# First chunk's softmax of taps issued ahead of the weights' loads, last four tokens in twos, and a new order of steps

## The chip, the cores and the metric

The kernel runs on one core of one Trainium2 chip. The metric is the device time in microseconds (us); the kernel before takes 1347.68 us (median of 3 runs, 1347.58 to 1349.73). Five engines work from queues of their own: PE (matrix products; PEld is its loading of weights), DVE (vector), ACT (scalar functions), POOL (GpSimd) and SP, which here only issues transfers. Each engine takes its instructions in the order in which they were written into its queue.

## The reference, cut to what matters

```
w   = softmax(weight_gen, axis=-1)            # 8 x 4160 x 8 heads x 7 taps
x   = einsum(w, last 7 rows of x_in)          # causal, 24 columns per head, 192 in all
h   = x @ w_in                                # 33280 x 192 by 192 x 1024
s   = h * softmax(h, axis=-1)
ln  = (s - mean(s)) / sqrt(var(s) + 1e-6) * g_ln
out = ln @ w_out                              # 33280 x 1024 by 1024 x 192
```

## The kernel before, in words

The 33280 rows are cut into 128 runs of 260, one run on each partition. A *token* t (0 to 259) is one row of every run, so one token is one 128-row tile of the products. Tokens are loaded in *chunks* that start at 0, 4, 12, 20, 36 and then every 16 up to 244.

For each chunk there is a softmax of the taps in seven steps (`softmax_taps`, t0 to t6): DVE takes the maximum (L112), POOL subtracts it (L114), ACT takes the exponential (L118), DVE sums (L120), ACT copies (L122), DVE takes the reciprocal (L124) and POOL multiplies (L126). For each *group* of tokens POOL then forms the seven products and adds them in part (attA and attB: L174, L180, L182 into `half`), DVE makes the last sum (fin, L433, into `a`) and ACT copies some columns (dup, L439). A group is 4 tokens; only the first four tokens go in two groups of 2 (`group`).

For each pair of tokens PE transposes `a` (xT, L450), ACT rounds it (xhi, L458) and DVE makes the rest (xld, L479, into `x_lo`). For each token follow, in this order: mm1 on PE (L491, L494 into a slot `h` of three in PSUM), max on DVE (L505), exp on ACT (L509), solu on DVE (L515), hi on ACT (L528), sq on ACT (L521), lo on DVE (L532), tr (a transposing transfer issued by SP, L540, `hlT`), mm2 on PE (L580) and out on ACT (L591). Steps sq and lo of one token never run at once. mm1 of token t needs sq and lo of token t-3. The scales of the output (f0 to f5, three small steps on ACT and three on DVE, L552 to L567) are made for 4 tokens at a time, for 2 among the first eight (`stat_group`); a store (L594) follows each fourth token.

At the start the weights come in as 64-bit numbers in `raw_a`, `raw_b` and `raw_2` and are converted in seven parts (a0, b, a1, c0 to c3) on DVE and ACT, L241 to L260, 512 or 384 columns each. Loads are issued on the queues of SP and of ACT (L76 to L90, L96, L195, L196, L202, L206). The steps of chunk 0's softmax of taps are written at L227, behind all of these loads.

From L640 on the steps are issued in the order that `issue_order` returns. It is a planner: each step has an engine, a cost in ns, and the steps it needs; some have a time before which they are not taken up (`ready`), each engine has a time at which it is free first (`free`), and among the steps that an engine could take the one with the smallest t + `URGENCY` goes first. The planner's order becomes the order of each engine's queue.

Of the kernel before, what the change touches and what calls it, by code (L numbers as in the profile page):

```python
# [26 lines left out]
def tile_kernel(ctx: ExitStack, tc: tile.TileContext, x, weight_gen, w_in, w_out, g_ln, out):  # L27
# [9 lines left out]
    RUN = B * S // P  # L37
    PB = P // B
    TG = 4
# [27 lines left out]
    def load_x(c, part=0):  # L67
        t0, n = starts[c], starts[c + 1] - starts[c]
        if part == 0:
            xs[c] = io.tile([P, (TC + HALO) * D], F32, name="xt")  # L70
        xt = xs[c]
        xv = xt.rearrange("p (t d) -> p t d", d=D)
        if c == 0:

            nc.gpsimd.memset(xt[:, : HALO * D], 0.0)
            nc.sync.dma_start(xv[:, HALO : HALO + n, :], x_run[:, :n, :])  # L76
            for b in range(B):
                queue = nc.sync if b % 2 else nc.scalar
                queue.dma_start(
                    xv[b * PB + 1 : (b + 1) * PB, :HALO, :],  # L80
                    x_run[b * PB : (b + 1) * PB - 1, RUN - HALO :, :],
                )
        elif t0 < HALO:
            first = xs[0].rearrange("p (t d) -> p t d", d=D)
            nc.sync.dma_start(xv[:, HALO : HALO + n, :], x_run[:, t0 : t0 + n, :])
            nc.sync.dma_start(xv[:, :HALO, :], first[:, t0 : t0 + HALO, :])
        else:
            cuts = [(HALO + n) * k // LOADS for k in range(LOADS + 1)]
            r0, r1 = cuts[part], cuts[part + 1]
            nc.sync.dma_start(xv[:, r0:r1, :], x_run[:, t0 - HALO + r0 : t0 - HALO + r1, :])  # L90
# [9 lines left out]
    TAP_STEPS = 7  # L100

    def softmax_taps(c, step):
        n = (starts[c + 1] - starts[c]) * H
        w3 = ws[c][:, : n * K].rearrange("p (n k) -> p n k", k=K)
        if step == 0:
            m = small.tile([P, TC * H], F32, name="wm", bufs=2)[:, :n]
            y = small.tile([P, TC * H], F32, name="wy", bufs=2)[:, :n]
            taps[c] = m, y
        m, y = taps[c]
        wide = [P, n, K]  # L110
        if step == 0:
            nc.vector.tensor_reduce(m, w3, axis=AX.X, op=ALU.max)  # L112
        elif step == 1:
            nc.gpsimd.tensor_tensor(  # L114
                out=w3, in0=w3, in1=m.unsqueeze(2).broadcast_to(wide), op=ALU.subtract
            )
        elif step == 2:
            nc.scalar.activation(w3, w3, AF.Exp)  # L118
        elif step == 3:
            nc.vector.tensor_reduce(m, w3, axis=AX.X, op=ALU.add)  # L120
        elif step == 4:
            nc.scalar.activation(y, m, AF.Copy, bias=1e-9)  # L122
        elif step == 5:
            nc.vector.reciprocal(y, y)  # L124
        elif step == 6:
            nc.gpsimd.tensor_tensor(  # L126
                out=w3, in0=w3, in1=y.unsqueeze(2).broadcast_to(wide), op=ALU.mult
            )
# [59 lines left out]
    w_in = w_in.bitcast(I32)  # L188
    w_out = w_out.bitcast(I32)
    load_x(0)  # L190
    raw_a = att.tile([P, 2 * FF], I32, name="raw_a", bufs=1)

    raw_b = big.tile([P, FF], I32, name="hl", bufs=3)
# [29 lines left out]
    column = const.tile([P, 1], F32, name="column")  # L223
    minus = const.tile([P, P], F32R, name="minus")
    nc.vector.tensor_scalar_mul(minus, ident, -1.0)

    for step in range(TAP_STEPS):  # L227
        softmax_taps(0, step)

    scratch = {}  # L230

# [173 lines left out]

    def stat_group(t):

        n = 2 if t < 2 * TG else TG
        return n if t % n == n - 1 else 0


    def group(t):

        if t < TG:
            return 2 if t % 2 == 0 else 0
        return TG if t % TG == 0 else 0

# [225 lines left out]


URGENCY = dict(
    a00=3.1, a01=2.3, a02=-28.9, a03=-6.5, a04=-3.6, a10=80, a11=-25.4, a12=-13, a13=-10, a14=10.4,
    attA=85.1, attB=2.4, b0=120.9, b1=-144.6, b2=138.3, b3=-1.5, b4=54.3, c00=-28.1, c01=85.1,
    c02=6.8, c10=-25.3, c11=31.3, c12=-72.7, c20=99.4, c21=-5.6, c22=10.2, c30=-149.7, c31=-14.5,
    c32=-100.3, dup=52.6, exp=-129.5, f0=8.2, f1=-120.4, f2=-71.5, f3=-118.4, f4=-66.1, f5=-45.6,
    fin=18.4, hi=-11, lo=33, lw=18.7, lx0=10.2, lx1=-115.4, lx2=-109.1, lx3=-20.7, max=-30,  # L650
    mm1=25.5, mm2=0.4, n0=-7.5, n1=11.8, n2=-1.8, n3=-113.6, n4=-8.6, n5=-69, n6=-123.6, od=-6.9,
    out=-81.2, p30=22.9, p31=0.5, p4=9.7, p5=12.6, p6=11.6, p70=-10.2, p71=-8.7, p80=20.3, p81=5.9,
    q00=7.1, q01=-5.1, q02=118.9, q10=-15.7, q11=20.7, q12=16.8, q20=100.6, q21=-95.2, q22=20.4,
    q30=143.8, q31=81.5, q32=98.3, solu=-7.6, sq=5, t0=5.1, t1=-3.7, t2=77.9, t3=44.1, t4=-26.5,
    t5=110.1, t6=267.2, tr=-13, v00=170.9, v01=5.1, v02=44, v03=0.2, v1=54.2, v2=58.8, v3=-12.2,
    v4=1, v5=21.2, xT=-66.9, xhi=-46.7, xld=30,
)


def issue_order(run, starts, group, stat_group, loads):  # L660
# [5 lines left out]

    PE, DVE, ACT, SP, POOL = range(5)
    SAME, CROSS = (25, 127, 143, 0, 102), 130
    free = [3000, 5900, 5000, 12000, 9050]
    steps, number = [], {}  # L670

    def add(name, t, engine, cost, *after, ready=0):
# [3 lines left out]
    def once(name, engine, cost, *after, ready=0):  # L676
        add(name, 0, engine, cost, *((x, 0) for x in after), ready=ready)
# [2 lines left out]
    parts = ["a0", "b", "a1", *(f"c{f}" for f in range(4))]  # L680
    for n, part in enumerate(parts):
        w_in, size = n < 3, 512 if n < 3 else 384
        at = (9000, 10500, 12000)[n] if w_in else 15000
        before = () if w_in else (f"{parts[n - 3]}4", "n" + {"a0": "0", "a1": "1", "b": "2"}[parts[n - 3]]) if n < 6 else ("q00",)
        if n:
            before += (parts[n - 1] + "0",)
        once(part + "0", DVE, 3 * (60 + size), *before, ready=at)
        once(part + "1", ACT, 2 * (190 + 0.85 * size), part + "0")
        once(part + "2", DVE, 3 * (60 + 1.04 * size), part + "1")
        if w_in:  # L690
            once(part + "3", ACT, 190 + 0.75 * size, part + "2")
            once(part + "4", DVE, 60 + 1.04 * size, part + "3")
            once("n" + {"a0": "0", "a1": "1", "b": "2"}[part], DVE, 60 + 1.04 * size, part + "2")
        else:
            f = n - 3
            once(f"q{f}0", ACT, 700, part + "2")
            once(f"q{f}1", PE, 660, f"q{f}0", *([f"q{f - 1}1"] if f else ["n6"]))
            once(f"q{f}2", ACT, 520, f"q{f}0")
    add("p30", 0, DVE, 868, ("q31", 0), ("mm1", 1))
# [31 lines left out]
        add("v4", t, DVE, 80, ("v3", t))  # L731
        add("v5", t, ACT, 240, ("v4", t))

    add("v00", 0, ACT, 1800, ready=9000)
    add_norms(0, 0)
    for c in range(1, len(starts) - 1):
        t, before = starts[c], starts[c - 1] if c > 1 else -1
        short = starts[c + 1] - t < 16
        if c > 1:
            add("lw", t, SP, 1270, last_group(c - 3))  # L740
            add("lx0", t, SP, 1540, last_group(c - 2), *parts_of(c - 2))
            for n in range(1, loads):
                add(f"lx{n}", t, SP, 1540, (f"lx{n - 1}", t))
        whole = starts[c + 1] - t == 16
        for part in range(4 if whole else 1):
            size = 830 if whole else 1800
            if c > 1:

                load = min(part + 1, loads - 1) if whole else loads - 1
                add(f"v0{part}", t, ACT, size, (f"lx{load}", t))  # L750
            else:
                add(f"v0{part}", t, ACT, size, ready=15000)
        add_norms(c, t)
        n = (starts[c + 1] - t) * 8
        on = (DVE, POOL, ACT, DVE, ACT, DVE, POOL)
        wide = 60 + 7.3 * n
        costs = (wide, 13.5 * n, 100 + 6 * n, wide, 100 + n, 60 + 6.3 * n, 13.5 * n)
        for k in range(7):
            if k:
                add(f"t{k}", t, on[k], costs[k], (f"t{k - 1}", t))  # L760
            elif c > 1:
                add("t0", t, on[k], costs[k], ("lw", t), ("t6", before))
            else:
                add("t0", t, on[k], costs[k], ready=12000)


    groups = [t for t in range(run) if group(t)]
# [1 line left out]
    for i, t in enumerate(groups):  # L769
        c, full = chunk_of(t), group(t) == 4  # L770
        after = [("attB", groups[i - 1])] if i else []
        if c:
            after.append(("t6", starts[c]))
        if c > 1:
            after.append((f"lx{loads - 1}", starts[c]))
        add("attA", t, POOL, 14990 if full else 7500, *after, ready=15000 if c == 1 else 9000)
        add("attB", t, POOL, 3510 if full else 1800, ("attA", t), ("fin", groups[i - 2] if i > 1 else -1))
        old = t // 4 * 4 - 12
        add("dup", t, ACT, 307 if full else 200, ("fin", t))
        add("fin", t, DVE, 1710 if full else 880, ("attB", t), ("xT", old + 2 if old >= 0 else -1))  # L780
# [144 lines left out]
```

## Time and profile before

| | |
|---|---|
| median of 3 runs | 1347.68 us |
| the profiled execution | 1347.67 us, of which the span from first to last instruction is 1345.8 us |
| granted PE clock, mean | 0.994 |
| max of token 0 starts at | 50.59 us |
| POOL's last sum (L182) starts at | 1286.95 us, 3.48 us long |
| last store issued at | 1342.58 us |

A row of the waits view reads "engine line waited for: total us, times, longest us". A row of a timeline reads "start, duration, engine, line, operation, out<-in, shapes, count, and in brackets the idle time ahead of it with what ended it"; ACTq and SPq rows are issues of transfers. A row of the windows view gives a stretch in us, its length, the busy time of PE, PEld, DVE, ACT and POOL (with counts), the granted PE clock, the busy share of the transfer engines and GB/s.

### The profile page before, as it was taken

What the parts mean: (1) busy time and instruction counts of PE and PEld (TensorE: products, weight loads), DVE (VectorE), ACT (ScalarE), POOL (GpSimd) and SP (SyncE); (2) the same over time, 40 slices, a digit from 0 to 9 for tenths busy, and PEclk for the clock granted to TensorE, in tenths of its full rate; (3) what the DMA queues carried; (4) which work ended last, traced back from release to release, by engine and by line L of the source; (5) the groups of instructions that cost most, each with busy time, mean ns of one, the idle gap of its engine ahead of it and who ended that gap; (6) DMA issues with size and microseconds to landing.
All of it is one profiled execution on the core that took longest, in us unless ns stands there. A gap on an engine that the chain in (4) does not pass through costs nothing.

```text
span 1345.8 us, 25810 instructions
## 1 busy us (share of the span) xinstructions
PE 1246.8 (93%) x9900; PEld 970.8 (72%) x9900; DVE 1210.2 (90%) x1588; ACT 1162.8 (86%) x2318; POOL 1247.7 (93%) x241
## 2 busy tenths in 40 slices
PE   0588899999999999999999999999999999999997
PEld 0365677777777777777777777777777777777776
DVE  5988899999999999999999999999999999889994
ACT  3778889889898988989898998989898898988886
POOL 5989899999999999999999999999999999999930
PEclk9899999999999999999999999999999999999999
DMA  5277668797886889688797968878787877976776
GB/s 180 74 159 169 139 134 201 123 207 137 155 179 134 196 137 208 125 179 163 129 202 140 191 140 180 162 128 203 140 193 137 183 150 138 183 134 123 133 134 130
DMA packets 565307, 210.31 MB, mean 156 GB/s; under 512 B 544456, under 2 KB 545864, under 8 KB 565184
## 3 DMA queue, kind: packets, MB, share of 16 engines
q1 hardware_dynamic: 563208, 206.55, 75.7%
q10 hardware_dynamic: 1976, 2.12, 0.6%
q8 instruction: 78, 1.28, 0.4%
q14 instruction: 45, 0.37, 0.1%
HBM read 46.15 MB, written 25.56 MB: 53 GB/s over the span
## 4 chain that ended last, share of the span: by engine, by line
ACT 43%; DVE 35%; issue 11%; PE 7%; DMA 2%; POOL 1%; SPq 0%; ACTq 0%; POOLq 0%
ACT hl L528 12%; ACT e L521 12%; DVE h L515 11%; DVE hl L532 11%; ACT e L509 9%; DVE stats L505 5%; DVE a L433 4%; ACT junk L145 3%; PE po L580 3%; PE h L494 2%; ACT x_hi L458 2%; ACT ot L591 2%; DMA hlT<-hl 2%; PE h L491 1%; DVE x_lo L479 1%
## 5 line engine op out<-in xcount | busy, mean ns | idle before, releaser
L174 POOL TENSOR_TENSOR pr<-xt,wt 128x5376 f32<-128x5376 f32 (+1 forms) x66 | 631.6, 9569 | 2.7
L580 PE MATMUL po<-w_hl,hlT 128*128 128x192 f16 x6192 | 555.1, 246 | 17.3 <-ACT ot L591 12.6
L580 PEld LDWEIGHTS <-hlT 128*128 128x128 f16 x6240 | 505.9, 98 | 83.2 <-issue 75.5
L515 DVE SCALAR_TENSOR_TENSOR h<-h,row,e 128x1024 f32<-128x1024 f32 x260 | 333.8, 1285 | 19.1 <-ACT e L509 16.9
L528 ACT ACTIVATE hl<-h 128x1024 f16<-128x1024 f32 x260 | 266.0, 1029 | 98.4 <-DVE h L515 55.4
L532 DVE SCALAR_TENSOR_TENSOR hl<-h,hl 128x1024 f16<-128x1024 f32 x260 | 316.5, 1218 | 36.8 <-ACT e L521 34.4
L180 POOL TENSOR_TENSOR pr<-pr 128x2304 f32<-128x2304 f32 (+1 forms) x66 | 333.0, 5045 | 5.2
L505 DVE TENSOR_REDUCE stats<-h 128x1 f32<-128x1024 f32 x260 | 316.3, 1217 | 3.9 <-PE h L494 3.3
L509 ACT ACTIVATE e<-h,stats 128x1024 f32<-128x1024 f32 x260 | 293.3, 1128 | 16.1 <-DVE stats L505 15.5
L521 ACT ACTIVATE e<-h,stats 128x1024 f32<-128x1024 f32 x260 | 293.0, 1127 | 1.1 <-DVE hl L532 1.0
L494 PE MATMUL h<-wa_hi,x_hi 128*128 128x512 f32 x520 | 234.0, 450 | 0.0
L182 POOL TENSOR_TENSOR half<-pr 128x1536 f32<-128x1536 f32 (+1 forms) x66 | 225.8, 3421 | 5.2
L494 PE MATMUL h<-wa_lo,x_hi 128*128 128x512 f32 x520 | 206.4, 397 | 0.0
L494 PE MATMUL h<-wa_hi,x_lo 128*128 128x512 f32 x520 | 205.9, 396 | 0.0
L494 PEld LDWEIGHTS h<-wa_hi,x_hi 128*128 128x128 f32 x520 | 98.1, 189 | 107.1 <-issue 95.5
L491 PE MATMUL h<-wb_hi,x_hi 64*128 64x512 f32 x520 | 131.0, 499 | 17.1 <-DVE hl L532 11.2
L433 DVE TENSOR_REDUCE a<-half 128x768 f32<-128x1536 f32 (+1 forms) x66 | 117.2, 1776 | 0.0
L591 ACT ACTIVATE ot<-po,stats 128x192 f32<-128x192 f32 x258 | 112.4, 436 | 3.6 <-PE po L580 3.6
L494 PEld LDWEIGHTS h<-wa_hi,x_lo 128*128 128x128 f32 x520 | 98.4, 189 | 23.2
L494 PEld LDWEIGHTS h<-wa_lo,x_hi 128*128 128x128 f32 x520 | 99.0, 190 | 12.0
L491 PE MATMUL h<-wb_hi,x_lo 64*128 64x512 f32 x520 | 104.2, 395 | 0.0
L450 PE MATMUL pa<-ident,a 128*128 128x128 f32 x520 | 81.2, 278 | 23.9 <-DVE x_lo L479 13.2
(89 smaller groups left out, 1072.0 us busy)
## 6 DMA issues: line engine op xcount, KB each, us to landing
out_dram<-ot SPq DMA_DIRECT2D x65, 384.0 KB, 3.3
xt<-in_x_dram SPq DMA_DIRECT2D x30, 576.0 KB, 4.8
xt<-in_x_dram SPq DMA_DIRECT2D x30, 480.0 KB, 4.4
wt<-in_weight_gen_dram SPq DMA_DIRECT2D x15, 448.0 KB, 4.8
hlT<-hl SPq DMA_TRANSPOSE x260, 4.7
xt<-in_x_dram SPq DMA_DIRECT2D x3, 384.0 KB, 4.6
raw_a<-in_moe_w_in_dram ACTq DMA_DIRECT2D x2, 512.0 KB, 7.4
raw<-in_moe_w_out_dram ACTq DMA_DIRECT2D x1, 768.0 KB, 12.2
```

Of the source, the lines that this page charges most:

```text
L174: nc.gpsimd.tensor_tensor(out=window(pr, 0, [(TG * D, K), (HG, n * H), (1, HG)]), in0=window(xt, t * D, [(D, K), (HG, n * H), (1, HG)]), i ...
L180: nc.gpsimd.tensor_tensor(out=pr[:, :3], in0=pr[:, :3], in1=pr[:, 3:6], op=ALU.add)
L182: nc.gpsimd.tensor_tensor(out=half, in0=window(pr, 0, [(2 * TG * D, 2), (D, n), (1, D)]), in1=window(pr, TG * D, [(5 * TG * D, 2), (D, n), ...
L491: nc.tensor.matmul(h[:, fs], lhs[rows, 1, :], rhs[rows], start=n == 0, stop=False)
L494: nc.tensor.matmul(h[:, fs], lhs[:, 0, :], rhs[:, fs], start=False, stop=n == 2)
L505: nc.vector.tensor_reduce(stat(t, NMAX), h_of[t], axis=AX.X, op=ALU.max, negate=True)
L509: nc.scalar.activation(e, h_of[t], AF.Exp, bias=stat(t, NMAX), accum_out=stat(t, Z))
L515: nc.vector.scalar_tensor_tensor(out=h, in0=h, scalar=row(t, SCALE), in1=e, op0=ALU.mult, op1=ALU.mult, accum_out=stat(t, M))
L521: nc.scalar.activation(e_of.pop(t), h_of[t], AF.Square, bias=stat(t, M), scale=-float(FF), accum_out=stat(t, Q),)
L528: nc.scalar.activation(hl[:, 0, :], h_of[t], AF.Copy, scale=2.0**14)
L532: nc.vector.scalar_tensor_tensor(out=hl[:, 1, :], in0=h_of[t], scalar=2.0**14, in1=hl[:, 0, :], op0=ALU.mult, op1=ALU.subtract,)
L580: nc.tensor.matmul(po[:, :D], hlT[:, half * NJ + j, :], w2_hl[:, j, w, :], start=n == 0, stop=n == len(terms) - 1,)
```

## The change

It has three parts. (1) The loop over chunk 0's seven tap steps is written directly behind `load_x(0)`, ahead of the loads of the weights. (2) `group` and `stat_group` give 2 for the last four tokens: POOL's products, DVE's last sum and ACT's copy run in two groups of 2 there, and so do the scales. (3) The table `URGENCY` gets other numbers throughout, the planner's first free times of DVE, ACT and POOL and the times at which loads are counted as landed are set anew, and the scaling q0 of the second weights now also waits for the conversion steps a02 and a12.

```diff
     load_x(0)
+    for step in range(TAP_STEPS):
+        softmax_taps(0, step)
     raw_a = att.tile([P, 2 * FF], I32, name="raw_a", bufs=1)
...
-
-    for step in range(TAP_STEPS):
-        softmax_taps(0, step)
...
     def stat_group(t):
-        n = 2 if t < 2 * TG else TG
+        n = 2 if t < 2 * TG or t >= RUN - TG else TG
...
     def group(t):
-        if t < TG:
+        if t < TG or t >= RUN - TG:
...
 URGENCY = dict(
-    a00=3.1, a01=2.3, a02=-28.9, a03=-6.5, a04=-3.6, a10=80, a11=-25.4, a12=-13, a13=-10, a14=10.4,
+    a00=109.7, a01=-3.8, a02=-82.9, a03=-5.2, a04=9.6, a10=51, a11=87.1, a12=-47.7, a13=-29.7,
...
-    free = [3000, 5900, 5000, 12000, 9050]
+    free = [3000, 5600, 7700, 12000, 6200]
...
-        at = (9000, 10500, 12000)[n] if w_in else 15000
+        at = (12000, 12000, 12500)[n] if w_in else 20000
...
-            once(f"q{f}0", ACT, 700, part + "2")
+            once(f"q{f}0", ACT, 700, part + "2", "a02", "a12")
...
-    add("v00", 0, ACT, 1800, ready=9000)
+    add("v00", 0, ACT, 1800, ready=10000)
...
-                add(f"v0{part}", t, ACT, size, ready=15000)
+                add(f"v0{part}", t, ACT, size, ready=21500)
...
-                add("t0", t, on[k], costs[k], ready=12000)
+                add("t0", t, on[k], costs[k], ready=15500)
...
-        add("attA", t, POOL, 14990 if full else 7500, *after, ready=15000 if c == 1 else 9000)
+        add("attA", t, POOL, 14990 if full else 7500, *after, ready=21500 if c == 1 else 10000)
```

In the changed kernel lines from 230 on stand one lower than before (L504 is max, L531 lo), and the lines of the loads two higher.

The first place is the head of ACT's queue. Before, the four loads of weights (two of `raw_a`, one of `raw_2`, named raw_101, and `g`) stand ahead of the exponential of the taps (`wt<-wt`):

```order
L79 DMA xt<-in_x_dram 15x1152 x4
L195 DMA raw_a<-in_moe_w_in_dram 128x1024 x2
L202 DMA raw_101<-in_moe_w_out_dram 128x4x384
L206 DMA g<-in_moe_g_ln_dram 128x8x1
L118 ACTIVATE wt<-wt 128x224
L145 ACTIVATE junk,squares_x<-xt 128x1920
L122 ACTIVATE wy<-wm 128x32
```

The same place in the changed kernel:

```order
L79 DMA xt<-in_x_dram 15x1152 x4
L197 DMA raw_a<-in_moe_w_in_dram 128x1024
L118 ACTIVATE wt<-wt 128x224
L197 DMA raw_a<-in_moe_w_in_dram 128x1024
L122 ACTIVATE wy<-wm 128x32
L204 DMA raw_110<-in_moe_w_out_dram 128x4x384
L208 DMA g<-in_moe_g_ln_dram 128x8x1
L145 ACTIVATE junk,squares_x<-xt 128x1920
```

The exponential moved ahead of the second `raw_a` load, and the copy of the sums (`wy<-wm`) ahead of `raw_2`, `g` and the squares of x.

The second place is POOL's queue from the first group of products on (`pr<-xt,wt` 7x384 is a group of two tokens, 5376 one of four; `wt<-wt,wm` and `wt<-wt,wy` of 448 are steps t1 and t6 of chunk 1). Before:

```order
L174 TENSOR_TENSOR pr<-xt,wt 128x7x384
L180 TENSOR_TENSOR pr<-pr 128x3x384
L182 TENSOR_TENSOR half<-pr 128x2x384
L114 TENSOR_TENSOR wt<-wt,wm 128x448
L174 TENSOR_TENSOR pr<-xt,wt 128x7x384
L180 TENSOR_TENSOR pr<-pr 128x3x384
L182 TENSOR_TENSOR half<-pr 128x2x384
L126 TENSOR_TENSOR wt<-wt,wy 128x448
L174 TENSOR_TENSOR pr<-xt,wt 128x5376
```

The same place in the changed kernel:

```order
L174 TENSOR_TENSOR pr<-xt,wt 128x7x384
L180 TENSOR_TENSOR pr<-pr 128x3x384
L182 TENSOR_TENSOR half<-pr 128x2x384
L174 TENSOR_TENSOR pr<-xt,wt 128x7x384
L180 TENSOR_TENSOR pr<-pr 128x3x384
L182 TENSOR_TENSOR half<-pr 128x2x384
L114 TENSOR_TENSOR wt<-wt,wm 128x448
L126 TENSOR_TENSOR wt<-wt,wy 128x448
L174 TENSOR_TENSOR pr<-xt,wt 128x5376
```

Chunk 1's step t1 moved behind the second group, so that t1 and t6 now stand next to each other.

The third place is DVE's queue at tokens 65 to 67, one of the repeating stretches in the middle of the run (max is `stats<-h`, solu `h,stats<-h,row,e`, lo `hl<-h,hl`, the last sum `a<-half`, the sum of the taps `wm<-wt`). Before:

```order
L505 TENSOR_REDUCE stats<-h 128x1
L552 TENSOR_REDUCE stats<-stats 128x4
L151 TENSOR_REDUCE row<-squares_x 128x1
L433 TENSOR_REDUCE a<-half 128x4x192
L515 SCALAR_TENSOR_TENSOR h,stats<-h,row,e 128x1024
L505 TENSOR_REDUCE stats<-h 128x1
L532 SCALAR_TENSOR_TENSOR hl<-h,hl 128x1024 x2
L515 SCALAR_TENSOR_TENSOR h,stats<-h,row,e 128x1024
L162 RECIPROCAL row<-row 128x1
L479 TENSOR_TENSOR x_lo<-pa,x_hi 128x512
L505 TENSOR_REDUCE stats<-h 128x1
L120 TENSOR_REDUCE wm<-wt 128x128
```

The same place in the changed kernel:

```order
L504 TENSOR_REDUCE stats<-h 128x1
L151 TENSOR_REDUCE row<-squares_x 128x1
L551 TENSOR_REDUCE stats<-stats 128x4
L432 TENSOR_REDUCE a<-half 128x4x192
L514 SCALAR_TENSOR_TENSOR h,stats<-h,row,e 128x1024
L504 TENSOR_REDUCE stats<-h 128x1
L531 SCALAR_TENSOR_TENSOR hl<-h,hl 128x1024
L120 TENSOR_REDUCE wm<-wt 128x128
L514 SCALAR_TENSOR_TENSOR h,stats<-h,row,e 128x1024
L478 TENSOR_TENSOR x_lo<-pa,x_hi 128x512
L504 TENSOR_REDUCE stats<-h 128x1
L531 SCALAR_TENSOR_TENSOR hl<-h,hl 128x1024 x2
```

Before, the lo of tokens 64 and 65 come together behind the max of token 66; in the changed kernel only that of 64 does, the sum of the taps follows it, and the lo of 65 waits until behind the max of token 67.

On PE, mm2 of tokens 9 to 12 stands behind mm1 of tokens 15, 16, 16 and 17 before, and behind mm1 of tokens 14, 14, 15 and 16 in the changed kernel; from token 14 on the distance is five tokens in both.

More of the change, by code (lines that the diff above doesn't have):

```diff
@@ L645 @@
 URGENCY = dict(
-    a00=3.1, a01=2.3, a02=-28.9, a03=-6.5, a04=-3.6, a10=80, a11=-25.4, a12=-13, a13=-10, a14=10.4,
[L647 to L656, printed above, removed]
+    a00=109.7, a01=-3.8, a02=-82.9, a03=-5.2, a04=9.6, a10=51, a11=87.1, a12=-47.7, a13=-29.7,
+    a14=-134.9, attA=12.1, attB=-5.5, b0=-4.4, b1=-81.6, b2=204.5, b3=-113.3, b4=-2.9, c00=-24.9,
+    c01=-97.7, c02=-113.8, c10=-3.5, c11=7.6, c12=-1.1, c20=-142.7, c21=-2.6, c22=40.2, c30=-12.6,
+    c31=-103.2, c32=-51.2, dup=101.3, exp=-230.8, f0=-73, f1=-47.1, f2=-108.3, f3=-178.9,
+    f4=-147.8, f5=-27.2, fin=-107.8, hi=-34.4, lo=20.7, lw=26.6, lx0=-22.2, lx1=-111.1, lx2=-75.4,
+    lx3=-56.8, max=-13.5, mm1=149.9, mm2=-38, n0=-13.6, n1=190.1, n2=-7, n3=109.7, n4=19.4, n5=0.5,
+    n6=-56.1, od=41.6, out=-115.5, p30=-14.7, p31=-85.8, p4=-0.2, p5=18.4, p6=-6.9, p70=0.3,
+    p71=-13.7, p80=11.5, p81=33.5, q00=-23.8, q01=3.6, q02=25.3, q10=10.5, q11=115.6, q12=-1.5,
+    q20=52.2, q21=11.6, q22=-67.6, q30=-86.1, q31=-13.9, q32=14.7, solu=-25.3, sq=-33.7, t0=114.6,
+    t1=54, t2=71.6, t3=-14.5, t4=297.3, t5=8.5, t6=-25.5, tr=-13.4, v00=32.5, v01=37.5, v02=59.2,
+    v03=72.4, v1=-138.7, v2=181.9, v3=-67.3, v4=130.5, v5=7.1, xT=66.1, xhi=-100, xld=-26.9,
 )
```

## The prediction

> **What bounds the kernel now.** I read the page's busy shares first, then the chain that ended last, the windows by stage, and the waits of POOL and of PE. The first three lines are the page's head (span, busy us and share of each engine) and its chain by engine.
>
> ```profile
> span 1345.8 us, 25810 instructions
> PE 1246.8 (93%) x9900; PEld 970.8 (72%) x9900; DVE 1210.2 (90%) x1588; ACT 1162.8 (86%) x2318; POOL 1247.7 (93%) x241
> ACT 43%; DVE 35%; issue 11%; PE 7%; DMA 2%; POOL 1%; SPq 0%; ACTq 0%; POOLq 0%
> ```
>
> POOL and PE are equally busy, yet POOL holds 1% of the chain: what ends last runs through ACT, DVE and PE. The windows (columns: stretch, length, busy PE, PEld, DVE, ACT, POOL, PE clock, transfers) show where PE has room:
>
> ```profile
> 86.00:166.00 80.00, 68.41 (x516) 52.12 (x515) 71.46 (x96) 71.89 (x149) 72.33 (x15) 0.97 0.79 167
> 166.00:1160.00 994.00, 969.91 (x7767) 755.05 (x7766) 920.42 (x1185) 888.83 (x1764) 979.98 (x180) 1.00 0.81 163
> ```
>
> PE is idle for 11.6 of 80 us in the ramp and for 2.4% in the long middle (24.1 of 994). So the middle is nearly bound by PE, and the ramp is where time lies. POOL's own waits (longest first):
>
> ```profile
> POOL wt L126 <- DVE wy L124: 13.7, 2, 13.3
> POOL wt L114 <- DVE row L151: 6.3, 1, 6.3
> ```
>
> These are large, but no row of the waits has DVE waiting for POOL; time that POOL wins ends in POOL's lead unless something behind it was late for POOL's sake.
>
> **Part 1, the first softmax.** The timeline of the start:
>
> ```profile
> 6.06 0.94 ACTq L195 DMA_DIRECT2D raw_a<-in_moe_w_in_dram  x2
> 8.86 0.39 ACT L118 ACTIVATE wt<-wt 128x224 f32<-128x224 f32 x1 [6.84 <-issue]
> 9.15 1.79 ACT L145 ACTIVATE junk<-xt 128x1920 f32<-128x1920 f32 x1
> 12.38 0.69 DVE L241 TENSOR_SCALAR h<-raw_a 128x512 int32<-128x512 int32 x1 [9.09 <-DMA raw_a<-in_moe_w_in_dram]
> 15.77 0.38 DVE L120 TENSOR_REDUCE wm<-wt 128x32 f32<-128x224 f32 x1
> 17.08 0.58 POOL L126 TENSOR_TENSOR wt<-wt,wy 128x224 f32<-128x224 f32 x1 [13.26 <-DVE wy L124]
> 17.73 4.95 POOL L174 TENSOR_TENSOR pr<-xt,wt 128x2688 f32<-128x2688 f32 x1
> 39.17 9.71 POOL L174 TENSOR_TENSOR pr<-xt,wt 128x5376 f32<-128x5376 f32 x1
> ```
>
> The exponential waits behind ACT's issues, and the sum behind DVE's conversion, which itself waits for `raw_a` until 12.38. In the new order the exponential follows the first `raw_a` issue (half of 0.94 from 6.06): about 6.5 to 6.9. The sum is then free of the conversion, and from the sum to POOL's multiply it takes 17.08 - 15.77 = 1.3, so POOL multiplies at about 8.2 and is done at 8.8. Its products also need all of x; ACT read that at 9.15 without a wait on a transfer, so x is there by then. First products: between 8.8 and 9.2 instead of 17.73, **8.5 us earlier**. The second `raw_a` issue slips by the exponential's 0.39, `raw_2` and `g` by a little more; DVE takes the second half of `raw_a` only after six or more conversion steps, which covers it; uncovered it would cost at most 0.4 to 1.
>
> Most of this is given back. The two groups of two lay between 17.73 and 39.17, 21.4 us with two tap steps between them, some 19 without; POOL is ready for t1 at about 28. But t6 now stands right behind t1, and between them lie an exponential, a sum, a copy and a reciprocal, whose places on DVE are fixed. DVE starts converting at the same 12.38, since `raw_a`'s first issue hasn't moved. Ahead of the reciprocal of chunk 1 its new queue has 18 steps of 512 columns, 6 of 384, two last sums of two tokens, and ten steps of the size of a small sum:
>
> ```profile
> L244 DVE TENSOR_SCALAR h<-raw_a 128x512 int32<-128x512 int32 x2 | 1.4, 695 | 0.1
> L244 DVE TENSOR_SCALAR h<-raw 128x384 int32<-128x384 int32 x4 | 2.2, 561 | 0.1
> L433 DVE TENSOR_REDUCE a<-half 128x384 f32<-128x768 f32 x2 | 1.9, 954 | 0.0
> L120 DVE TENSOR_REDUCE wm<-wt 128x64 f32<-128x448 f32 x2 | 1.2, 610 | 0.0
> ```
>
> 18 x 0.695 + 6 x 0.561 + 2 x 0.954 + 10 x 0.61 = 23.9, so t6 at 36.3 with no gap, 37.3 with 0.03 between steps, and the first group of four starts at about 38.3 instead of 39.17: **1 us** is left of 8.5. And its last sum on DVE, which PE's next transpose awaits, is bound by DVE, not by POOL:
>
> ```profile
> 20.00:40.00 20.00, 3.07 (x10) 2.33 (x10) 17.04 (x34) 9.71 (x27) 19.19 (x9) 1.00 0.40 135
> 40.00:60.00 20.00, 9.41 (x42) 6.90 (x42) 18.21 (x33) 15.75 (x39) 19.84 (x5) 0.92 0.00 0
> 60.48 1.77 DVE L433 TENSOR_REDUCE a<-half 128x768 f32<-128x1536 f32 x1
> ```
>
> A group of four takes POOL 18.4 (869.77 - 0.42 - 849.16 - 1.77 in the rows of the middle, below), so POOL's part would be done at 38.3 + 18.4 = 56.7 (before 57.6), while DVE reaches the last sum at 60.48 after work that fills all but 4.8 of the 40 us. In the new order the same work stands ahead of it, and one sum of taps (0.61) more. So this term lies between -4.2 (all of DVE's idle time gone) and +2 (that sum, and for a stall that the old order doesn't have the 1.3 that the chain from sum to multiply took above); I take **0**, as the order of the work around it hardly differs.
>
> The rows that follow show PE's clock around this point (8th number after the length).
>
> ```profile
> 53.00:62.40 9.40, 0.11 (x2) 0.05 (x2) 9.15 (x16) 9.06 (x18) 9.32 (x4) 0.71 0.19 35
> 62.40:66.00 3.60, 3.60 (x12) 2.23 (x13) 3.60 (x7) 2.76 (x11) 3.60 (x1) 0.50 0.29 54
> ```
>
> PE idles 9.3 us for this last sum and then works 3.6 us at half clock. The Trainium skill, "TensorE: Matmul & The Clock Gate", section "HAM oscillation — how this bites in real kernels", asks for no PE-idle gap above about 3.4 us; the trace agrees with that here. By that rule a gap closed below 3.4 would give another 3.6 / 2 = 1.8 us (an estimate from that page's rule and the row above), a gap that stays gives nothing. As the last sum stays at about 60, the gap stays.
>
> **Part 3 in the ramp (tokens 4 to 20).** PE's waits from 86 to 166 us:
>
> ```profile
> PE po L580 <- DMA hlT<-hl: 4.3, 3, 2.0
> PE po L580 <- ACT ot L591: 3.7, 2, 2.7
> PE h L491 <- DVE hl L532: 3.0, 2, 2.4
> ```
>
> 11.0 us, each a step queued earlier than its input comes. POOL also loses its 6.3 here; in the new queue two groups of four stand between t1 and t6 of chunks 3 and 4, so it waits less, but that feeds its lead. If the ramp ran with the middle's idle share, 2.4% of 80 = 1.9 of the 11.6, it would give 9.7. Against it, mm2 of tokens 9 to 12 now stands four or five tokens behind mm1 (before five or six), which leaves less time to the transposing transfer: three more waits of 2.0 would cost 6. The table is new for all of these steps, and I expect that a third of the 11.0 goes: **-3.7**, ends -9.7 and +6.
>
> **Part 3 in the middle.** There are 13 chunks of 16 tokens from 36 to 244. One of them (734 to 812 us) has these waits of PE, and POOL's rows give its length:
>
> ```profile
> PE pa L450 <- DVE x_lo L479: 0.5, 1, 0.5
> PE h L491 <- ACT e L521: 0.5, 1, 0.5
> PE h L491 <- DVE hl L532: 0.5, 1, 0.5
> ...
> 849.16 1.77 POOL L114 TENSOR_TENSOR wt<-wt,wm 128x896 f32<-128x896 f32 x1
> 869.77 1.77 POOL L126 TENSOR_TENSOR wt<-wt,wy 128x896 f32<-128x896 f32 x1 [0.42 <-DVE stats L552]
> 926.94 1.78 POOL L114 TENSOR_TENSOR wt<-wt,wm 128x896 f32<-128x896 f32 x1
> ```
>
> A chunk takes 77.78 us, and POOL waits 0.42 of it. So however good the new order is, POOL's own 77.36 is the next wall: at most 0.42 x 13 = **-5.5**. Where lo is put off past a last sum, the stall looks like this:
>
> ```profile
> 780.10 2.34 DVE L532 SCALAR_TENSOR_TENSOR hl<-h,hl 128x1024 f16<-128x1024 f32 x2
> 784.23 1.21 DVE L505 TENSOR_REDUCE stats<-h 128x1 f32<-128x1024 f32 x1
> ...
> 781.46 0.50 PE L491 MATMUL h<-wb_hi,x_hi 64*128 64x512 f32 x2 [0.47 <-DVE hl L532]
> 786.38 0.50 PE L491 MATMUL h<-wb_hi,x_hi 64*128 64x512 f32 x2
> ```
>
> The first lo ends at 781.3 and PE, which needed it, starts at 781.46, 0.5 late. In the new queue this lo stays, but the second goes behind the next max: it would end at 784.23 + 1.21 + 1.17 = 786.6, just past 786.38, 0.2 to 0.3 late. A second such place stands in each new chunk (0.5), while an old one, with solu put off, is gone (0.5), and the wait for `x_lo` may go or stay. Per chunk that is 0.25 less or 0.25 more; I take **0**, with +0.7 per chunk (+9) as the upper end, where each of three late lo costs some 0.25 more.
>
> **Part 2 and the end.** The tail in the timeline:
>
> ```profile
> 1286.95 3.48 POOL L182 TENSOR_TENSOR half<-pr 128x1536 f32<-128x1536 f32 x1
> 1333.98 1.78 SPq L540 DMA_TRANSPOSE hlT<-hl  x1
> 1342.58 0.34 SPq L594 DMA_DIRECT2D out_dram<-ot  x1
> ```
>
> POOL is done at 1290.4, 55 us before the end, so halving its last group (two of about 9.5 instead of one of 18.4) costs or gains nothing there; it would cost 0.6 if POOL's lead were gone. A few small steps of the scales come in on ACT and DVE beside PE's last products. The end hangs on the last transfer at 1333.98, its landing, one mm2, one out and the store; the last lo still stands behind the first of the last scales. **-0.3**, between -1 and +1.
>
> **Sum.** 0 - 3.7 + 0 - 0.3 = -4.0 on the profiled 1347.67 (1345.8 of span and 1.9 around it), which is the median too: **1343.7 us**.
>
> **Rivals.** (a) *POOL's gain goes through*: 8.5 at the start, 6.3 in the ramp and 5.5 in the middle are 20.3 us, 1327. It needs PE's side to be late because of POOL; against it stand POOL's 1% of the chain and the t6 wait above. 0.12. (b) *No change at the end*: every stall of the ramp is replaced by one alike and the middle stays: 1347.5. For it speaks that DVE's work from 12.38 to 60 is the same. 0.24. (c) *Slower*: the late lo. Three places in each of 13 chunks hold up mm1; with some 0.25 more each than counted above it is +9, less what the ramp brings: 1353. It decides once lo of the second token ends later than 786.6 in the picture above, that is, if ACT's hi or sq ahead of it slip by more than 0.3. 0.20. (d) The forecast, 0.44, between 1339 and 1346 by itself.
>
> Under (d) the time is faster by over 0.2% (2.7 us, about what a measurement can tell from no change) in nearly all cases: 0.40 of 0.44, so faster is 0.52, same 0.24 + 0.04 = 0.28, slower 0.20. The range leaves out the far part of (a) and of (c): 1331 to 1355.
>
> **What would show it.** Right: first products at about 9 us, POOL then idle for some 7 us ahead of the second t6, the group of four at about 38, its last sum at about 60, PE's gap ahead of it still there, less than 11.0 of waits in the ramp, chunks of 77.4 to 78.1 us. Wrong: chunks above 78.3 (c), a last sum of group 4 before 57, or DVE waiting for POOL (a).

## The result and the profile after

The changed kernel takes 1330.76 us (median of 4 runs, 1330.10 to 1331.18) against 1347.63 for the kernel before (4 runs): 0.9872 of it, 95% interval 0.9855 to 0.9889. That is 16.9 us less, where 4.0 less was forecast.

The head of the page of the changed kernel (span, busy us of each engine) and its chain by engine:

```profile
span 1328.9 us, 25783 instructions
PE 1242.2 (93%) x9900; PEld 969.3 (73%) x9900; DVE 1212.4 (91%) x1592; ACT 1155.3 (87%) x2323; POOL 1248.4 (94%) x244
POOL 52%; DVE 15%; ACT 14%; issue 10%; PE 7%; DMA 1%; POOLq 0%; ACTq 0%; DVEq 0%
```

POOL held 1% of the chain before and holds 52% now, with the same busy time (1247.7 before). The same two windows as before (busy PE is the first column behind the length), and the waits of POOL and of DVE:

```profile
86.00:166.00 80.00, 73.33 (x566) 56.49 (x564) 74.29 (x101) 73.81 (x154) 77.56 (x17) 0.98 0.82 162
166.00:1160.00 994.00, 973.47 (x7827) 760.77 (x7827) 930.68 (x1196) 894.05 (x1788) 983.88 (x180) 1.00 0.82 164
```

```profile
POOL wt L126 <- DVE wy L124: 11.0, 2, 6.4
POOL wt L114 <- DVE wm L112: 5.2, 4, 2.1
...
DVE a L432 <- POOL half L182: 5.8, 10, 0.7
```

PE's idle time in the ramp fell from 11.6 to 6.7 us. POOL's 6.3 us wait of the ramp is gone, and DVE now waits for POOL, which it did nowhere before. The timeline of the start, the last sum of the group of four, and one chunk of the middle by POOL's rows:

```profile
9.14 4.94 POOL L174 TENSOR_TENSOR pr<-xt,wt 128x2688 f32<-128x2688 f32 x1
...
36.06 0.97 POOL L126 TENSOR_TENSOR wt<-wt,wy 128x448 f32<-128x448 f32 x1 [6.38 <-DVE wy L124]
37.10 9.70 POOL L174 TENSOR_TENSOR pr<-xt,wt 128x5376 f32<-128x5376 f32 x1
58.48 1.77 DVE L432 TENSOR_REDUCE a<-half 128x768 f32<-128x1536 f32 x1
60.40 0.45 PE L449 MATMUL pa<-ident,a 128*128 128x128 f32 x1 [8.35 <-DVE stats L551]
...
838.42 1.75 POOL L114 TENSOR_TENSOR wt<-wt,wm 128x896 f32<-128x896 f32 x1
858.58 1.78 POOL L126 TENSOR_TENSOR wt<-wt,wy 128x896 f32<-128x896 f32 x1
915.82 1.76 POOL L114 TENSOR_TENSOR wt<-wt,wm 128x896 f32<-128x896 f32 x1
```

POOL's first products, its long wait and the start of the group of four lie where they were forecast; the last sum came 2.0 us earlier (60.48 before). A chunk takes 77.40 us (77.78 before), and POOL's 0.42 us of waiting in it is gone.

Where the 16.9 us lie is read from the start of max, one row for each token, counted through the timeline of DVE (us; in brackets the difference from before). The rows below the first two are experiments that follow.

| kernel | token 4 | 28 | 52 | 148 | 212 | 228 | 259 |
|---|---|---|---|---|---|---|---|
| before | 81.0 | 205.3 | 322.3 | 789.8 | 1100.6 | 1179.0 | 1325.9 |
| after | 77.7 (-3.3) | 196.4 (-9.0) | 312.4 (-10.0) | 776.1 (-13.7) | 1085.7 (-14.9) | 1162.6 (-16.4) | 1309.5 (-16.4) |
| e1, start alone | 77.8 (-3.2) | 201.0 (-4.3) | 318.0 (-4.3) | 785.4 (-4.4) | 1096.3 (-4.3) | 1174.9 (-4.1) | 1321.8 (-4.1) |
| e2, order alone | 79.3 (-1.7) | 198.0 (-7.4) | 314.0 (-8.3) | 778.0 (-11.8) | 1087.6 (-13.0) | 1164.7 (-14.3) | 1311.0 (-14.9) |
| e4, new ramp | 77.5 (-3.5) | 196.2 (-9.2) | 313.1 (-9.3) | 780.5 (-9.3) | 1091.6 (-9.0) | 1169.8 (-9.2) | 1316.5 (-9.4) |
| e5, new middle | 77.4 (-3.6) | 200.9 (-4.4) | 317.0 (-5.3) | 779.5 (-10.2) | 1088.7 (-12.0) | 1165.7 (-13.3) | 1312.5 (-13.4) |
| e9, no t1 | 74.7 (-6.3) | 193.6 (-11.8) | 309.5 (-12.8) | 772.0 (-17.8) | 1080.3 (-20.3) | 1157.0 (-22.0) | 1303.8 (-22.1) |

So the start gave 3.3, the ramp 5.7, the middle to token 212 5.9, the stretch to 228 another 1.4, and the end 0.5 (the last store starts at 1325.69, before at 1342.58). From one execution to the next the start moves by some us: over the seven kernels whose start is that of the changed one, max of token 4 lay between 76.1 and 79.0, so single profiles of the start are read with that in mind.

### The profile page after: what moved, and what is told of

It is laid out like the page before. It is cut to its first block, busy times and chain, and to the rows that moved or that the text cites. A ratio compares the mean times of both kernels' runs of the same rounds, so it can differ in the third digit from the quotient of the medians.

```text
span 1328.9 us, 25783 instructions
## 1 busy us (share of the span) xinstructions
PE 1242.2 (93%) x9900; PEld 969.3 (73%) x9900; DVE 1212.4 (91%) x1592; ACT 1155.3 (87%) x2323; POOL 1248.4 (94%) x244
## 4 chain that ended last, share of the span: by engine, by line
POOL 52%; DVE 15%; ACT 14%; issue 10%; PE 7%; DMA 1%; POOLq 0%; ACTq 0%; DVEq 0%
POOL pr L174 28%; POOL pr L180 15%; POOL half L182 6%; DVE h L514 5%; ACT e L520 5%; DVE hl L531 5%; ACT hl L527 4%; PE h L493 3%; ACT e L508 2%; PE po L579 2%; DVE stats L504 2%; DVE a L432 2%; PE h L490 1%; POOL wt L114 1%; POOL wt L126 1%
## 5 line engine op out<-in xcount | busy, mean ns | idle before, releaser
L531 DVE SCALAR_TENSOR_TENSOR hl<-h,hl 128x1024 f16<-128x1024 f32 x260 | 315.4, 1219 | 32.3 <-ACT e L520 30.9
L504 DVE TENSOR_REDUCE stats<-h 128x1 f32<-128x1024 f32 x260 | 316.4, 1218 | 9.0 <-PE h L493 8.7
L490 PEld LDWEIGHTS h<-wb_hi,x_hi 64*128 64x128 f32 x520 | 49.3, 184 | 75.5 <-issue 32.7
```

The lines of the kernel that those rows point to most:

```text
L490: nc.tensor.matmul(h[:, fs], lhs[rows, 1, :], rhs[rows], start=n == 0, stop=False)
L504: nc.vector.tensor_reduce(stat(t, NMAX), h_of[t], axis=AX.X, op=ALU.max, negate=True)
L531: nc.vector.scalar_tensor_tensor(out=hl[:, 1, :], in0=h_of[t], scalar=2.0**14, in1=hl[:, 0, :], op0=ALU.mult, op1=ALU.subtract,)
```

## The experiments

### Which part brings what: e1, e2, e3, e12

e1 is the kernel before with part 1 alone.

```diff
     load_x(0)
+    for step in range(TAP_STEPS):
+        softmax_taps(0, step)
...
-    for step in range(TAP_STEPS):
-        softmax_taps(0, step)
```

> The kernel before with part 1 alone (the first softmax of taps ahead of the loads; old table, old ends). Theory A (the new order of steps is what brought 16.9 us; the earlier start alone is given back at once): POOL's first products at about 9.1 instead of 17.73 us, but POOL then waits at chunk 1's t1 or t6, the group of four starts within 1 us of 39.17, and the time is 1345.5 to 1348 (0 to -2 us). Rival B (POOL's earlier start goes through): the group of four starts at 31 to 33 and the time is 1338 to 1341 (-7 to -9).

Measured 1345.46 us (ratio 0.9982, 0.9972 to 0.9992): 2.3 less than before, at the lower edge of Theory A's range. Its picture of POOL did not come. These are DVE and POOL in e1:

```profile
12.30 0.69 DVE L240 TENSOR_SCALAR h<-raw_a 128x512 int32<-128x512 int32 x1 [4.71 <-DMA raw_a<-in_moe_w_in_dram]
12.90 0.34 DVE L124 RECIPROCAL wy<-wy 128x32 f32<-128x32 f32 x1
...
13.98 4.95 POOL L174 TENSOR_TENSOR pr<-xt,wt 128x2688 f32<-128x2688 f32 x1
36.16 9.70 POOL L174 TENSOR_TENSOR pr<-xt,wt 128x5376 f32<-128x5376 f32 x1
```

In the old order the reciprocal of the taps still stands behind DVE's first conversion step, which waits for `raw_a`. So the first products start at 13.98, 3.75 us earlier than before and not the 8.6 expected, and the group of four starts 3.0 us earlier (36.16), not within 1 us of 39.17. Most of what POOL gains here goes through. In the profiled execution, the fastest of the ten (1343.74), max is 3.2 us ahead at token 4 and 4.1 at the end. The way lies through ACT's queue, first before, then in e1:

```profile
28.24 0.58 ACT L118 ACTIVATE wt<-wt 128x448 f32<-128x448 f32 x1 [4.69 <-POOL wt L114]
28.72 0.58 ACT L248 ACTIVATE h<-h 128x512 f32<-128x512 int32 x1
29.33 0.58 ACT L249 ACTIVATE h<-h 128x512 int32<-128x512 int32 x1
29.94 0.69 DVE L253 SCALAR_TENSOR_TENSOR frac<-raw_a,h 128x512 f32<-128x512 uint32 x1 [2.41 <-ACT h L249]
```

```profile
24.47 0.58 ACT L118 ACTIVATE wt<-wt 128x448 f32<-128x448 f32 x1 [0.92 <-POOL wt L114]
24.95 0.58 ACT L247 ACTIVATE h<-h 128x512 f32<-128x512 int32 x1
...
57.47 1.77 DVE L432 TENSOR_REDUCE a<-half 128x768 f32<-128x1536 f32 x1
```

Before, the exponential of chunk 1's taps stands at the head of ACT's queue and waits 4.69 us for POOL's t1; two conversion steps stand behind it, and DVE waits 2.41 us for them. With POOL earlier, ACT waits 0.92, DVE not at all, and the last sum of group 4 starts 3.0 us earlier (57.47 against 60.48). This is a way on which POOL's gain does go through. e1 does not show what the whole 8.5 us would bring in the old order; by this trace a still earlier POOL gains nothing more on this way, as DVE waits no longer.

e2 is the kernel before with part 3 alone: the new table and the new numbers of the planner.

```diff
-    a00=3.1, a01=2.3, a02=-28.9, ...
+    a00=109.7, a01=-3.8, a02=-82.9, ...
-    free = [3000, 5900, 5000, 12000, 9050]
+    free = [3000, 5600, 7700, 12000, 6200]
```

> The kernel before with part 3 alone (new table and new calibration of the planner; taps behind the loads, last group still of four). Theory A: the ramp and the middle gain as in the changed kernel, only the 3 us of the start are in doubt: 1331 to 1335, chunks of 77.4 us. Rival B: without the earlier start POOL is behind by up to 8 us where the ramp begins, and as POOL bounds the middle in the changed kernel, this stays to the end: 1337 to 1341, chunks of 77.4 us all the same.

Measured 1332.79 us (0.9884, 0.9870 to 0.9899), 15.0 less: Theory A. The ramp gains the same 5.7 us (-1.7 to -7.4) as in the changed kernel, and the middle settles at the same 77.4 us a chunk. Here DVE waits 2.22 us for POOL at the first last sum, so in the new order too the late POOL reaches DVE at the start; part 1 takes that away and is worth 2 to 3 us on top (1330.76 with all three parts, 1329.91 in e3, which has parts 1 and 3).

e3 is the changed kernel without part 2, e12 the kernel before with part 2 alone.

```diff
-        n = 2 if t < 2 * TG or t >= RUN - TG else TG
+        n = 2 if t < 2 * TG else TG
...
-        if t < TG or t >= RUN - TG:
+        if t < TG:
```

> The changed kernel without part 2 (the last four tokens and their scales together again). POOL's last group is then ready some 9 us later for tokens 256 and 257, with PE some 30 us behind POOL there. Theory A: no difference beyond 1 us, 1330 to 1332. Rival C (the halved last group is needed, as POOL now bounds the middle and its lead is gone): 1334 to 1340.

> The kernel before with part 2 alone (last group in twos, the last scales in twos). Theory A: POOL's last group lies some 4 us ahead of DVE and 20 us ahead of the products there, so nothing waits for it: 1346.5 to 1348.5. Rival C (the last four tokens wait for their group): 1340 to 1345.

Measured: e3 1329.91 us (1329.79 to 1331.24), e12 1349.01 beside 1348.22 for before (1.0001, 0.9991 to 1.0010). The twos change nothing that can be measured, with either order. e3 lies 0.1 us below the range of its Theory A; e12 lies 0.5 us above the range of both its theories and within the spread of the runs of before beside it (1346.92 to 1351.12).

### Ramp and middle apart: e4, e5

Both hold the old planner beside the new one and splice the two lists of steps at the first product of token 28 (`issue_order_old` is the old table with the old numbers); e5 has the two names the other way round.

```diff
-    for op, t in issue_order(RUN, starts, group, stat_group, LOADS):
+    head = issue_order(RUN, starts, group, stat_group, LOADS)
+    head = head[: head.index(("mm1", 28))]
+    rest = [s for s in issue_order_old(RUN, starts, group, stat_group, LOADS) if s not in set(head)]
+    for op, t in head + rest:
```

> The changed kernel (parts 1 and 2 in) with the new order only up to the first product of token 28; what is left follows in the old order. Theory A (ramp and middle gain each by itself): max of token 28 comes 9 us earlier than in the kernel before, chunks then take 77.8 us again with waits of PE for x_lo, e and ot, the stall near token 220 is back, and the time is 1337 to 1340 (-8 to -10). Rival D (the ramp makes POOL's lead and the lead makes the middle faster): chunks of 77.4 us although the order is the old one, 1331 to 1334.

> The changed kernel (parts 1 and 2 in) with the old order up to the first product of token 28 and the new one behind it. Theory A (ramp and middle gain each by itself): max of token 28 where it was before (within 2 us of 214.3), chunks of 77.4 us behind it, time 1339 to 1342 (-6 to -8). Rival E (what the ramp loses is made up in the middle, because PE has room there, 76.0 us of its own work in 77.4): 1331 to 1335.

Measured: e4 1338.80 us (0.9929, 0.9914 to 0.9944), e5 1335.33 (0.9913, 0.9898 to 0.9928). e4 is Theory A: 9.2 us at token 28 and 9.0 at 212, so the old order keeps its 77.8 a chunk (77.85 on average from token 68 to 228), with the same waits of PE for `x_lo`, e and ot as before. e5 lies between its theories, 0.3 us above the range of E: it starts the middle only 4.4 ahead of before and then makes up ground. These are max of tokens 52 and 148 in e5:

```profile
317.04 1.22 DVE L504 TENSOR_REDUCE stats<-h 128x1 f32<-128x1024 f32 x1
...
779.55 1.21 DVE L504 TENSOR_REDUCE stats<-h 128x1 f32<-128x1024 f32 x1
```

Six chunks in 462.5 us are **77.08 us a chunk**: the new order's own pace on PE's side while POOL is still ahead. POOL's 77.4 is slower. So the last sums follow POOL's part by 4.2 us at token 36 of e5, by 2.4 at 132, and by 1.5 from 180 on, where e5 has the pace of the changed kernel. From token 28 to the last, the new middle wins 9.0 us in e5 and 7.4 in the changed kernel: a late ramp is partly made up, until POOL's wall is reached. (The 8.9 us of e4 and the 12.2 of e5 can't be added, since both have the earlier start.)

PE's waits from 320 to 780 us show what the order did, before and in e5:

```profile
PE pa L450 <- DVE x_lo L479: 3.4, 7, 0.5
PE h L491 <- ACT e L521: 2.9, 6, 0.5
PE h L491 <- DVE hl L532: 2.3, 5, 0.5
PE po L580 <- ACT ot L591: 1.5, 4, 0.4
```

```profile
PE h L490 <- DVE hl L531: 7.3, 12, 0.8
```

The waits for the late lo are there as foretold (two in a chunk, up to 0.8), and all others are gone: 10.1 us became 7.3. That is 2.8 of the 4.9 us that the six chunks gained; the rest lies within PE's busy time (456.35 us before, 454.11 in e5).

### Is POOL the bound? e6, e7

Both add a fill on POOL to 16 chunks, e6 to the changed kernel, e7 to the kernel before.

```diff
-        pr = att.tile([P, K, TG, D], F32, name="pr", bufs=1)[:, :, :n]
+        pr = att.tile([P, K, TG, D], F32, name="pr", bufs=1)
+        if t == 0 and n == TG and xt is not xs[1]:
+            nc.gpsimd.memset(pr[:, 0, :, :].rearrange("p t d -> p (t d)"), 0.0)
+        pr = pr[:, :, :n]
```

> The changed kernel with one more fill of 128x768 on POOL (some 0.7 us by the 1.06 us of the 128x1152 fill at the start) ahead of the first products of 16 chunks (from token 12 on): work that nothing reads. Theory F (POOL is the bound of the middle now): each fill is paid nearly in full, chunks of 78.1 us, +9 to +11 us, 1340 to 1342. Rival G (POOL merely runs at the same pace as PE's side, which sets it): chunks stay at 77.4, 1330 to 1333.

> The kernel before with the same fills. Theory F (before, POOL waited 0.42 us in each chunk and its last sums lay 3.8 us ahead of DVE): of 0.7 us 0.42 goes into the wait, the 0.3 left use up the 3.8 us over the 14 chunks, and the time is 1347 to 1350 (0 to +2). Rival G' (POOL bound the middle before too): +9 to +11, 1357 to 1359.

Measured: e6 1341.97 us, 11.2 more than the changed kernel; e7 1349.97 against 1347.51 (1.0016, 1.0006 to 1.0025). A row of the fill in e6, and below it DVE's waits for POOL from 300 to 1100 us in e6 and in e7:

```profile
903.77 0.74 POOL L175 MEMSET pr<- 128x768 f32 x1
...
DVE a L435 <- POOL half L185: 13.5, 21, 1.0
```

```profile
DVE a L436 <- POOL half L185: 0.8, 3, 0.3
```

16 fills of 0.74 are 11.8 us: the changed kernel pays 11.2 of them, the kernel before 2.5, at the end of which its lead is used up (the last sums follow POOL by 0.2 us from token 164 on, 4.4 in the kernel before). Theory F in both. POOL bounds the middle now and did not before.

### What taking work off POOL brings: e9, e10, e8, e11, e13

e9 leaves out t1, e10 also the maximum t0.

```diff
-            nc.gpsimd.tensor_tensor(
-                out=w3, in0=w3, in1=m.unsqueeze(2).broadcast_to(wide), op=ALU.subtract
-            )
+            pass
```

> The changed kernel with step t1 (the subtraction of the maximum ahead of the exponential of the taps, 1.77 us of POOL in a chunk of 16) left out everywhere; the order is otherwise the same. Theory H (the new order's own pace on PE's side is 77.1 us a chunk: where the old ramp left PE behind POOL, max went from 317.0 at token 52 to 779.5 at token 148, 77.08 a chunk; POOL's 77.4 lies just above it): chunks of 77.1, 14 x 0.3 = 4 us less, 1325.5 to 1328. Rival I (PE's own 76.0 a chunk is what is behind POOL): 1311 to 1318.

> As the one without t1, with the maximum itself (step t0 on DVE, 1.08 us in a chunk of 16) left out too. If the new order's own pace is set by how much DVE has to do, chunks fall by up to 1.08 more against the run without t1, to 76.0 to 76.8: 1311 to 1323. If it is set by where the late lo stands in DVE's queue (0.80 and 0.42 us in each chunk, at places with no t0 ahead of them), the time is that of the run without t1, within 1 us: 1325 to 1328.

Measured: e9 1326.83 us (1325.49 to 1327.91), e10 1325.44 (1324.88 to 1325.61). Both run at 77.08 a chunk (309.5 to 772.0 from token 52 to 148 in e9), with POOL waiting again and the same waits of PE for lo:

```profile
851.25 1.77 POOL L124 TENSOR_TENSOR wt<-wt,wy 128x896 f32<-128x896 f32 x1 [1.32 <-DVE stats L549]
```

In its profiled execution e9 is 5.7 us ahead of the changed kernel at the end: 2.8 by token 28, of which the spread of the starts may be a part, and the rest in the middle. e10 is 1.4 us below e9, a little more than the 1 us expected, but its chunks are the same. So Theory H: the bound behind POOL is the new order itself, 0.3 us a chunk below it. It is not the amount of DVE's work, since t0's 1.08 us less in a chunk changes no chunk. From 320 to 780 us the only waits of PE that are left are those for the late lo (7.3 us, 12 times, in e5, e9 and e10 alike), so the place of lo in DVE's queue is the likely bound; no run moves it.

e8 keeps t1, but on DVE for all chunks of 16; e11 from token 36 on, e13 from 68 on.

```diff
-            nc.gpsimd.tensor_tensor(
+            (nc.vector if n == TC * H else nc.gpsimd).tensor_tensor(
                 out=w3, in0=w3, in1=m.unsqueeze(2).broadcast_to(wide), op=ALU.subtract
```

> The changed kernel with the subtraction of the maximum (step t1, 1.77 us of POOL in each chunk of 16 tokens) on DVE, at the same place of the order. Theory F (POOL is the bound now): POOL's own work falls to 75.6 us in a chunk, DVE has some 1.15 us more (its 128x512 tensor_tensor takes 0.68), and chunks fall from 77.4 to between 76.0 (PE's own work) and 77.0: 1312 to 1326. Rival G (PE's and DVE's order sets the pace and POOL only follows): DVE's extra 1.15 us is paid in part, chunks of 77.4 to 78.5, 1331 to 1346.

Measured 1342.67 us, 11.9 more than the changed kernel: in the range of Theory G, but by neither theory's mechanism. Of this, 10.6 us stand at token 20 already, ahead of the middle. DVE's first t1 and POOL's rows beside it:

```profile
78.64 6.90 DVE L114 TENSOR_TENSOR wt<-wt,wm 128x896 f32<-128x896 f32 x1
...
74.88 9.71 POOL L174 TENSOR_TENSOR pr<-xt,wt 128x5376 f32<-128x5376 f32 x1
84.67 5.80 POOL L180 TENSOR_TENSOR pr<-pr 128x2304 f32<-128x2304 f32 x1
```

POOL's products end at 84.59, DVE's t1 at 85.54, 0.95 later; and POOL's next sum lasts 5.80 instead of 5.12.

> The changed kernel with t1 on DVE, but only for the chunks from token 36 on. Theory J (the 12 us lost by t1 on DVE everywhere came at two places of the ramp, where DVE's t1 lasted 6.90 and 3.81 us beside a running product of POOL instead of some 0.9; in the middle it began 0.7 us before POOL's instruction ended and the chunks took 77.29): the ramp is that of the changed kernel, chunks 77.3, 1328 to 1330. Rival K (t1 on DVE harms the middle too): 1333 to 1340.

Measured 1339.96 us, at the edge of Rival K, but the middle is Theory J's (77.27 a chunk) and the loss is again in the ramp: chunk 36's t1 comes as early as 121.46 us and lasts 8.93, for which Theory J had no term. PE waits 7.9 us there, and its clock is at half for 13.7 us from 127.0 on.

> The changed kernel with t1 on DVE for the chunks from token 68 on, the first of them with its t1 at about 218 us. Theory L (DVE's t1 and a running instruction of POOL exclude each other: in the run with t1 on DVE from token 36, DVE's t1 lasted 8.93 us beside POOL's products, which had 8.0 us to go, and POOL's next instruction lasted 0.7 longer): at 218 us POOL has 1.2 us of its last sum left, so DVE loses 1.2 + 0.95 = 2.1 us once, the ramp stays that of the changed kernel (max of token 36 within 2 us of 235.3), chunks take 77.3, nothing is won: 1331 to 1334. Rival M (the 8.93 us had to do with something else of the ramp, and POOL is really relieved by 1.77 us in a chunk): chunks of 77.1 as in the run without t1, 1326 to 1329.

Measured 1330.78 us, the time of the changed kernel, 0.2 below Theory L's range and 1.8 above M's. DVE's first t1 there, and POOL beside it:

```profile
215.71 3.35 DVE L114 TENSOR_TENSOR wt<-wt,wm 128x896 f32<-128x896 f32 x1
...
214.62 3.49 POOL L182 TENSOR_TENSOR half<-pr 128x1536 f32<-128x1536 f32 x1
218.19 10.44 POOL L174 TENSOR_TENSOR pr<-xt,wt 128x5376 f32<-128x5376 f32 x1
```

t1 stands until POOL's instruction ends at 218.11 and ends 0.95 later; then chunks take 77.28. Against the changed kernel e13 loses 1.9 us between tokens 28 and 36 and wins back 0.7 by the end; that both end together rests on the 1.2 us by which this execution is ahead at token 28, behind a ramp in which PE's clock never fell to half (for 3.4 us in the changed kernel). No version tried that computes the whole reference is measurably faster than the changed kernel.

## Why the prediction was wrong, point by point

**The start.** POOL's part was right to within 1.2 us: products at 9.14 (8.8 to 9.2 forecast), 6.38 of waiting (some 7), the group of four at 37.10 (38.3); DVE's conversion began at 12.76, 0.4 us later than the 12.38 taken. The term for its last sum was taken as 0, because "DVE reaches the last sum at 60.48 after work that fills all but 4.8 of the 40 us". The step that failed is the 4.8: I took this idle time as given, and did not ask what ended it. 2.41 of it hung on POOL through ACT's queue (e1), the queue that the changed kernel reorders. The last sum came at 58.48, and with part 1 alone at 57.47; forecast "about 60". PE's gap ahead of it stayed, as forecast (8.35 us). What closing it below 3.4 us would have brought is not shown, and the estimate of 1.8 us rests on too simple a rule: in both kernels PE's clock also fell to half for 3.4 us behind waits of 2.2 and 2.4 us, though not behind one of 2.7 (at 146.97 before).

**The ramp.** The mechanism was right in part and the size was off: "a third of the 11.0" (-3.7) was measured as 5.7, in e2 without the new start too. Counted by tokens, from max of token 4 to max of token 20, PE's waits fell from 13.7 to 9.5 us. The term had these waits alone and nothing for PE's clock, though a stretch at half clock went too. These are the long wait and PE's windows before (columns: stretch, length, busy PE, clock, transfers), then the same in the changed kernel:

```profile
128.52 0.80 PE L491 MATMUL h<-wb_hi,x_hi 64*128 64x512 f32 x2 [2.44 <-DVE hl L532]
84.00:88.00 4.00, 3.84 (x12) 0.57 1.04 290
128.60:132.00 3.40, 3.40 (x11) 0.51 0.99 173
```

```profile
89.60 0.50 PE L490 MATMUL h<-wb_hi,x_hi 64*128 64x512 f32 x2 [2.24 <-DVE hl L531]
91.00:95.00 4.00, 4.00 (x22) 0.57 1.24 165
128.60:132.00 3.40, 3.21 (x34) 1.00 0.41 149
```

Before, two stretches of 3.4 us at half clock lie in the ramp (from 84.2 and 128.6), now one (from 91.1). The runs with the old ramp (e1, e5, e7, e12) have two or three there, those with the new one (e2, e3, e4, e6, e9, e10) one. By the row above, one stretch less is worth some 3.4 / 2 = 1.7 us, an estimate. From 100 to 122 us PE has no wait left, where 3.8 us of waits for the transposing transfer stood before. The fear that a shorter distance between mm1 and mm2 makes more such waits was wrong there; between 78 and 100 us they went from 0.6 to 1.3.

**The middle.** This term failed by most: 0 taken, 5.9 measured to token 212. The wall was right ("POOL's own 77.36 is the next wall"; 77.40 measured), and so were the late lo. The most that the wall allows was taken too small, as "at most 0.42 x 13": the last sums also moved closer behind POOL's part, which they follow by 4.4 us before and by 1.6 now at token 212 (3.1 and 2.5 at token 36). What failed is the balance of +0.25 or -0.25 a chunk. It set a new stall of 0.5 against an old one and let the wait for `x_lo` go or stay, but the waits for `x_lo`, e and ot all went, 7.8 of the 10.1 us in six chunks. By itself the order gains 0.7 a chunk (77.08 in e5 and e9 against 77.78), and POOL's wall stopped it at 0.4. The 1.4 us between tokens 212 and 228 were in no term: max of token 224 comes 6.9 us after that of 223 before and in 6.7 in e4, which has the old order there, but in 4.7 in the changed kernel.

**The end.** -0.3 forecast, about -0.5 measured, and nothing of it from the twos (e3, e12).

**The rivals.** Rival (a), "POOL's gain goes through" with 1327, is nearest in number, at a chance of 0.12, and mostly wrong in its reason. At the start some of POOL's gain did go through (e1: first products 3.75 us earlier, the time 2.3 less). In the ramp and the middle it was not POOL that had held PE back: adding POOL work to the kernel before costs little (e7), and the earlier start does not change the old order's chunks (e1, e4). Its sign, DVE waiting for POOL, came all the same, like POOL's 52% of the chain; both are signs of a PE side that got faster. Rival (c), the late lo, happened in two places of each chunk and cost less than what left. The range failed at its lower end because it joined terms that each had a known best case (-4.2, -9.7, -5.5, -1) as if they could not come near it together: their sum is -20.4, and -16.9 came.

## What to carry to other kernels

A small wait that repeats in each chunk beside an engine with a fixed sum of work gives a wall; where the order of all steps is new, the time can end at the wall, as here, so it is not only the best case, and the price of one foretold stall is to be set against all the waits that the old order has there. The idle time of an engine that seems bound by its own queue is to be followed through the queue that feeds it, since an in-order engine hands on a wait for a third one. When a faster side meets its wall, adding work to the suspect in both kernels shows at once which of them it bounds.

## What the runs showed of the hardware

A subtraction on DVE whose operands both lie in SBUF (where the kernel's tiles lie) did not run beside POOL's instruction. It lasted 6.90, 8.93 and 3.35 us in the rows above, and all 41 of them in e8, e11 and e13 ended 0.94 to 0.96 us after the end of the POOL instruction that ran when they started, whether that was a product or a sum. POOL's next instruction was then 0.7 us longer (10.44 instead of 9.71 for the products). DVE's steps that read one operand from PSUM, where PE's products lie, kept their durations beside POOL: in the changed kernel max and lo took 1.20 to 1.23 us in the middle and 1.21 to 1.23 after POOL's last instruction. The Trainium skill, "SBUF — State Buffer", section "Who interferes with whom", says that a DVE instruction with two inputs in SBUF contends with a GpSimd instruction that reads SBUF, and that this contention is an exclusive lock; the trace agrees. Moving t1 from POOL to DVE therefore does not free all of its time on POOL here: of the 1.77 us of t1 some 0.7 came back in the next products. POOL then waits again (some 0.7 us in a chunk of e13), so the 77.28 a chunk are the pace of PE's side with t1 in DVE's queue.
